# Scores taken from one pair transpose of q and k, the first units' low parts moved to ScalarE, and the last decisions moved by one slot

## Chip, core and metric

One core of a Trainium2 chip runs the whole program. The metric is device time in microseconds: the median of the runs of the kernel before is 1012.94 (1012.55 to 1014.28, three runs).

## The reference

Three layers, one after the other, all in float32 (the dense weights arrive as float64):

```
scores = q @ k.T / sqrt(64);  keep = (key < 4) | (0 <= query - key < 128)     # 4 sinks, window 128
x = softmax(where(keep, scores, -1e9)) @ v          # 4 batches, 8 heads, 768 positions, head size 64
x = (x @ w1) * (x @ w2) @ w3 @ w_out                # x: 3072 tokens x 512
logits = x @ w_gate + modality_bias[modality_id]; e = argmax(logits); gate = softmax(logits)[e]
out = gate * (relu(x @ w1[e]) @ w2[e])              # 8 experts, 512 -> 1024 -> 512, one per token
```

## The kernel before

Nearly every product is done in three passes of float32r: a high part (rounded by ScalarE as it copies) and a low part (the rest, by VectorE) of each operand, high x high, high x low and low x high.

**Start.** `startup_stream` loads the float64 weights with SP's DMA queue, builds float32 of them with three VectorE operations each (L182, L185, L188), transposes w3 on TensorE (L280) and multiplies w3 by w_out (L289). Attention of the first units runs between these.

**Attention.** The 3072 queries are 12 units of 256 (three to a batch), each with 4 pairs of heads: 48 steps n. For one n, `att_stream` yields five times: scores of the unit's first 128 queries, `a_scores(n, 0)`; sink weights and transposed P of n-1, `a_sk` and `a_pt`; q of n+1, `a_tq` and `a_swap`; scores of the second 128 queries; P times V of n-1, `a_pv`, and k of n+1, `a_tk`. Before a transpose, `a_split` lays the high and low part of a head side by side, so that one 128x128 transpose gives 64 rows of high part over 64 of low part; `a_swap` makes a copy with these halves exchanged. A score is then two products over 128 rows: (high, low) with (high, low), and the swapped pair with the same (L441). q takes four transposes and k four (L396, L415). What is kept of the previous unit's k lies in `carry`, and the sinks' k in `ksk`. P is divided by its sum on VectorE (L468). P times V (L531) is in full float32 and writes 64 output rows for one head and the other 64 for its partner. `defer` puts a VectorE step one yield later (`tick`).

**Dense layer.** `moe1_stream` takes two units at a time, six groups: L703 for x @ w1 and x @ w2, L691 for the product with w3 x w_out. During group g, attention of group g+1 and routing of group g-1's units run between: `route` is a generator of sixteen dot products on VectorE (L764) and the bookkeeping after them, among which five small matmuls (L786 to L790) wait for the one-hot rows of L775. How fast it is stepped is the `due` line of `front`.

**Experts.** `back` works through slots of 512 tokens. `decide` finds on VectorE, in some 16 tiny operations, which expert has most tokens left; SP reads the answer into registers and then issues the loads of token numbers (L846) and of the expert's weights (L868, L870), all on one queue. Four slots are decided early, in the last dense group; two more and one of 128 tokens are decided when all tokens are routed, at slot 2 (`pos == N_EARLY - 2`). A slot is `stage1` (L912), then four `stage2` (L949); within the latter stand the next slot's `w1_piece` splits and its transposes (L899).

A scheduler sets the order of each engine's instructions from the program's order, its own costs and the waits; engines then run their lists strictly in order.

Of the kernel before, what the change touches and what calls it, by code (L numbers as in the profile page):

```python
# [26 lines left out]
def attention_moe_moe_kernel(ctx, tc, q, k, v, w1, w2, w3, w_out, mod_id, w_gate, mod_bias, e_w1, e_w2, out,  # L27
                             n_sink, window, dbg=None):
    nc = tc.nc
# [16 lines left out]
    banded = n_sink == NS and window == 128  # L46

# [46 lines left out]
    neg_r = const.tile([128, 128], F32R, name="neg_r")  # L94
    cur_i = const.tile([128, 128], I32, name="cur_i")
# [12 lines left out]
    ksk = const.tile([128, H, NS], F32R, name="ksk")  # L108
# [3 lines left out]
    def consts_early():  # L112
# [5 lines left out]
        nc.vector.tensor_scalar(out=neg_r, in0=idf, scalar1=-1.0, scalar2=None, op0=ALU.mult)  # L118
        nc.gpsimd.memset(tmp, 1.0)
# [217 lines left out]
    carry = {}  # L337
    xb = mm.tile([128, NP, 2, 3, UNIT], F32R, tag="xb", bufs=1, name="xb")

    def a_load(n):  # L340
        u, p = divmod(n, NP)
        b, c = divmod(u, NC)
        hs = slice(2 * p, 2 * p + 2)
        qn = att.tile([128, 2, 2, D], F32, tag="qn", bufs=2, name="qn")
        kn = att.tile([128, 2, 2, D], F32, tag="kn", bufs=2, name="kn")
        for src, dst in ((q, qn), (k, kn)):
            for j in range(2):
                s0 = c * UNIT + j * 128
                nc.sync.dma_start(out=dst[:, :, j], in_=src[b, hs, s0:s0 + 128, :].rearrange("h s d -> s h d"))
        nat[n] = (qn, kn)  # L350

    def a_load_v(n):
# [3 lines left out]
        vn = att.tile([128, 3, 2, D], F32, tag="vn", bufs=2, name="vn")  # L356
# [4 lines left out]
        if c == 0 and p == 0:  # L361
            for kind in range(3):
                for h in range(2):
                    r = kind * 32 + h * NS
                    nc.sync.dma_start(out=vst[r:r + NS, :, h * D:(h + 1) * D],
                                      in_=v[b].rearrange("(p h) s d -> h s p d", h=2)[h, 0:NS])
# [7 lines left out]
    def a_split(n):  # L374
        qn, kn = nat.pop(n)
        qs = att.tile([128, 4, 2, D], F32R, tag="qs", bufs=1, name="qs")
        ks = att.tile([128, 4, 2, D], F32R, tag="ks", bufs=1, name="ks")
        qf = qn.rearrange("p h j d -> p (h j) d")
        kf = kn.rearrange("p h j d -> p (h j) d")
        nc.scalar.activation(out=qs[:, :, 0, :], in_=qf, func=ACTF.Copy, scale=1.0 / float(D) ** 0.5)  # L380
        nc.scalar.activation(out=ks[:, :, 0, :], in_=kf, func=ACTF.Copy)

        def low_parts():
            nc.vector.scalar_tensor_tensor(out=qs[:, :, 1, :], in0=qf, scalar=1.0 / float(D) ** 0.5,
                                           in1=f32(qs[:, :, 0, :]), op0=ALU.mult, op1=ALU.subtract)
            nc.vector.tensor_tensor(out=ks[:, :, 1, :], in0=kf, in1=f32(ks[:, :, 0, :]), op=ALU.subtract)

        stt["low", n] = defer(low_parts)
        stt["s", n] = (qs, ks)

    def a_tq(n):
        qs, ks = stt["s", n]
        stt.pop(("low", n))()
        tp = ps_t.tile([128, 4, 128], F32R, tag="t", name="tq")
        for i in range(4):
            nc.tensor.transpose(out=tp[:, i, :], in_=qs[:, i].rearrange("p a d -> p (a d)"), identity=idr)  # L396
        qT = att.tile([128, 4, 128], F32R, tag="qT0", bufs=2, name="qT")
        nc.scalar.activation(out=qT, in_=f32(tp), func=ACTF.Copy)
        stt["q", n, 0] = qT
        stt["tq", n] = tp  # L400

    def a_swap(n):
        qW = att.tile([128, 4, 128], F32R, tag="qT1", bufs=2, name="qW")
        tp = stt.pop(("tq", n))
        for x in range(2):
            nc.scalar.activation(out=qW[x * D:(x + 1) * D], in_=f32(tp[(1 - x) * D:(2 - x) * D]), func=ACTF.Copy)
        stt["q", n, 1] = qW

    def a_tk(n):
        u, p = divmod(n, NP)  # L410
        b, c = divmod(u, NC)
        qs, ks = stt.pop(("s", n))
        tp = ps_t.tile([128, 4, 128], F32R, tag="t", name="tk")
        for i in range(4):
            nc.tensor.transpose(out=tp[:, i, :], in_=ks[:, i].rearrange("p a d -> p (a d)"), identity=idr)  # L415
        kT = att.tile([128, 2, 3, KW], F32R, tag="kT", bufs=1, name="kT")
        for h in range(2):
            nc.scalar.activation(out=kT[:, h, 1:3, NS:KW], in_=f32(tp[:, 2 * h:2 * h + 2, :]), func=ACTF.Copy)
        if c == 0:
            nc.gpsimd.tensor_copy(out=ksk[:, 2 * p:2 * p + 2, :], in_=f32(kT[:, :, 1, NS:2 * NS]))  # L420
        s0 = 0 if c else 1
        nc.gpsimd.tensor_copy(out=kT[:, :, s0:3, 0:NS],
                              in_=f32(ksk[:, 2 * p:2 * p + 2, :]).unsqueeze(2).to_broadcast([128, 2, 3 - s0, NS]))
        if c:
            nc.vector.tensor_copy(out=kT[:, :, 0, NS:KW], in_=f32(carry[p]))
        if c < NC - 1:
            cr = att.tile([128, 2, 128], F32R, tag=f"carry{p}", bufs=1, name="carry")
            nc.vector.tensor_copy(out=cr, in_=f32(kT[:, :, 2, NS:KW]))
            carry[p] = cr
        stt["k", n] = kT  # L430

    def a_scores(n, j):
        u, p = divmod(n, NP)
        b, c = divmod(u, NC)
        kT = stt["k", n]
        sp = ps_s.tile([128, 2, 512], F32, tag="s", name="sp")
        blk0 = c == 0 and j == 0
        s0 = 1 if blk0 else j
        for h in range(2):
            for part in range(2):  # L440
                nc.tensor.matmul(out=sp[:, h, 0:2 * KW], lhsT=stt["q", n, part][:, 2 * h + j, :],  # L441
                                 rhs=kT[:, h, s0:s0 + 2, :].rearrange("p a b -> p (a b)"),
                                 start=(part == 0), stop=(part == 1))
# [8 lines left out]
        else:  # L452
            nc.vector.copy_predicated(out=sp[:, :, NS:KW], mask=cur_i.unsqueeze(1).to_broadcast([128, 2, 128]),
# [10 lines left out]
        def norm():  # L464
            r = st[:, 2]
            nc.vector.tensor_scalar(out=st[:, 1], in0=st[:, 1], scalar1=1.0e-9, scalar2=None, op0=ALU.add)
            nc.vector.reciprocal(out=r, in_=st[:, 1])
            nc.vector.tensor_tensor(out=P[:, j, :, lo:KW], in0=P[:, j, :, lo:KW],  # L468
# [4 lines left out]
    def a_sk(n):  # L473
# [6 lines left out]
        xp = ps_x.tile([128, 2, 256], F32, tag="x", name="xp")  # L480
        stt["x", n] = xp
# [5 lines left out]
        for j in range(j0, 2):  # L487
# [3 lines left out]
                                    op=ALU.subtract)  # L491
            nc.tensor.transpose(out=xp[0:96, 1, j * 128:(j + 1) * 128].bitcast(F32R), in_=psk[:, j, :], identity=idr)
# [25 lines left out]
    def a_pv(n):  # L518
# [10 lines left out]
        for x, (vj, cols, pm) in enumerate(spans):  # L529
            for h in range(2):  # L530
# [4 lines left out]
                         start=False, stop=True, skip_group_check=True)  # L535
        xh, xl = xb[:, p, 0, u % 3], xb[:, p, 1, u % 3]
        nc.scalar.activation(out=xh, in_=xp[:, 0], func=ACTF.Copy)  # L537
        defer(lambda: nc.vector.tensor_tensor(out=xl, in0=xp[:, 0], in1=f32(xh), op=ALU.subtract))
        stt.pop(("k", n)); stt.pop(("q", n, 0)); stt.pop(("q", n, 1))

    NN = NU * NP

    att_done = [0]
    ATT_STEPS = 5

    def att_stream():
        a_load(0)
        a_load_v(0)
        a_load(1)
        a_vsink(0)  # L550
        a_split(0)
        a_tq(0)
        a_swap(0); yield
        a_tk(0); yield
# [660 lines left out]
```

## Time and profile before

| | us |
|---|---|
| median of the runs shown | 1012.94 |
| profiled execution, its own time | 1017.59 |
| span of its profile | 1015.9 |
| dense groups 0 to 5 begin at | 129.3, 227.6, 332.3, 432.8, 531.5, 632.5 |
| slots 0 to 5 begin at | 708.7, 754.6, 800.7, 855.3, 901.2, 947.0 |
| last matmul begins | 1003.4 |

The page gives busy time and idle time; a timeline gives the start and length of runs of like instructions. The length of a TensorE row has a modelled end, so that rows overlap: what a piece of TensorE work costs is read from one start to the next start. In L531's rows a float32 matmul stands as two instructions, one for each pass over its columns.

### The profile page before, as it was taken

The numbers are of one execution on the slowest core, as the hardware profiler recorded it, in microseconds if no ns is written. First come the engines' busy times: TensorE is split into PE (matmuls) and PEld (weight loads), VectorE is DVE, ScalarE is ACT, GpSimd is POOL, SyncE is SP. The second block draws the span as 40 slices with busy tenths as digits, with TensorE's granted clock in tenths as the row PEclk, the third lists the DMA queues.
The fourth block names the chain that finished last, engine by engine and source line by source line (L and its number), as shares of the span: only waits on it lengthen the run. The fifth ranks groups of instructions, "written<-read, shape, count | busy, mean of one in ns | idle before, by whom it ended". The sixth has DMA issues, their size and how long they took to land. (4 is left out here: it accounts for less than half of the span.)

```text
span 1015.9 us, 16038 instructions
## 1 busy us (share of the span) xinstructions
PE 956.0 (94%) x4976; PEld 752.5 (74%) x4976; DVE 644.0 (63%) x1968; ACT 515.8 (51%) x1354; POOL 218.0 (21%) x460
## 2 busy tenths in 40 slices
PE   4899799999999999999999999999999997999995
PEld 2667578867786778678867886778888886888884
DVE  7788796489638963895489639847934354343432
ACT  3689665576447644774576445314433414343433
POOL 1232312113223221222122222222031222021010
PEclk9899999999999999999999999999999998999998
DMA  8665624112202220222022200452445306343331
GB/s 262 188 171 167 188 69 131 23 45 63 58 19 49 58 55 19 56 61 52 16 50 59 58 9 16 129 80 63 145 166 117 133 13 236 125 146 117 122 116 52
DMA packets 125417, 94.05 MB, mean 93 GB/s; under 512 B 96712, under 2 KB 105160, under 8 KB 125201
## 3 DMA queue, kind: packets, MB, share of 16 engines
q1 hardware_dynamic: 120560, 80.12, 28.3%
q0 software_dynamic: 4768, 12.88, 4.2%
q8 instruction: 40, 0.66, 0.3%
q14 instruction: 49, 0.39, 0.2%
HBM read 80.14 MB, written 13.09 MB: 92 GB/s over the span
## 5 line engine op out<-in xcount | busy, mean ns | idle before, releaser
L703 PE MATMUL ab<-xb,wab 128*128 128x512 f32 x1152 | 291.0, 397 | 0.4 <-DVE g L713 0.3
L703 PEld LDWEIGHTS ab<-xb,wab 128*128 128x128 f32 x1152 | 210.6, 189 | 41.9 <-ACT xb L537 1.2
L949 PE MATMUL x<-w 128*128 128x512 f32 x600 | 143.1, 396 | 0.0
L764 DVE CUSTOM_DVE_ANT_0 junk<-rows,wgb 128x512 bf16<-128x512 f32 x192 | 134.8, 702 | 1.5 <-ACT rows L751 0.6
L949 PEld LDWEIGHTS x<-w 128*128 128x128 f32 x600 | 113.1, 190 | 23.7 <-DVE w L196 0.3
L691 PE MATMUL x2p<-w3o,gh 128*128 128x512 f32 x384 | 128.2, 407 | 0.0
L461 ACT ACTIVATE P<-sp,st 128x132 f32<-128x132 f32 (+1 forms) x192 | 69.2, 368 | 40.4 <-DVE st L459 26.4
L196 DVE TENSOR_TENSOR w<-wst,w 128x512 fp32r<-128x512 f32 x112 | 71.5, 683 | 25.1 <-ACT w L195 25.1
L513 POOL TENSOR_SCALAR_AFFINE_SELECT ptp<-ptf 128x512 f32<-128x512 f32 (+1 forms) x96 | 63.7, 688 | 107.8 <-ACT ptf L508 107.8
L691 PE MATMUL x2p<-w3o,gl 128*128 128x512 f32 x192 | 76.4, 400 | 0.0
L691 PEld LDWEIGHTS x2p<-w3o,gh 128*128 128x128 f32 x384 | 66.9, 188 | 11.8 <-ACT gh L680 1.9
L912 PE MATMUL ab<-w,w 128*128 128x512 f32 x288 | 75.1, 396 | 0.0
L916 DVE SCALAR_TENSOR_TENSOR w<-ab,w 128x512 fp32r<-128x512 f32 x48 | 33.1, 690 | 65.6 <-ACT w L915 65.4
L195 ACT ACTIVATE w<-wst 128x512 fp32r<-128x512 f32 x112 | 63.5, 628 | 20.9 <-DMA wst<-in_moe_w_dram 20.9
L912 PE MATMUL ab<-w 128*128 128x512 f32 x288 | 74.0, 392 | 0.0
L953 POOL DMA_INDIRECT out_dram<-late,ti x25 | 25.6, 1026 | 217.1 <-ACT late L952 193.0
L680 ACT ACTIVATE gh<-g 128x256 fp32r<-128x256 f32 x96 | 39.9, 415 | 63.0 <-DVE g L710 48.1
L710 DVE TENSOR_TENSOR g<-ab,bs 128x256 f32<-128x256 f32 x48 | 20.2, 421 | 76.6 <-PE ab L703 76.5
L485 POOL CAST psk<-P 128x16 fp32r<-128x16 f32 (+1 forms) x96 | 23.7, 276 | 202.1 <-DVE P L468 149.6
L915 ACT ACTIVATE w<-ab 128x512 fp32r<-128x512 f32 x48 | 28.8, 599 | 74.5 <-PE ab L912 74.1
L912 PEld LDWEIGHTS ab<-w,w 128*128 128x128 f32 x288 | 54.0, 188 | 13.0
L912 PEld LDWEIGHTS ab<-w 128*128 128x128 f32 x288 | 54.0, 188 | 12.1
(195 smaller groups left out, 1685.7 us busy)
## 6 DMA issues: line engine op xcount, KB each, us to landing
wst<-in_moe_w_dram SPq DMA_DIRECT2D x56, 512.0 KB
f64st<-in_moe_w_dram SPq DMA_DIRECT2D x32, 512.0 KB
vn<-in_v_dram SPq DMA_DIRECT2D x128, 64.0 KB
xs<-rows SPq DMA_DIRECT2D x12, 513.0 KB
qn<-in_q_dram SPq DMA_DIRECT2D x96, 64.0 KB
kn<-in_k_dram SPq DMA_DIRECT2D x96, 64.0 KB
f64st<-in_moe_w_out_dram SPq DMA_DIRECT2D x8, 512.0 KB
wgb<-wgt SPq DMA_DIRECT2D x1, 2048.0 KB
```

The lines of the kernel that those rows point to most:

```text
L195: nc.scalar.activation(out=hi, in_=src, func=ACTF.Copy)
L196: lo_eng.tensor_tensor(out=lo, in0=src, in1=f32(hi), op=ALU.subtract)
L461: nc.scalar.activation(out=P[:, j, h, lo:KW], in_=sp[:, h, lo:KW], func=ACTF.Exp, bias=st[:, 0, h:h + 1], accum_out=st[:, 1, h:h + 1])
L513: nc.gpsimd.affine_select(out=parts[:, a, i0:2].rearrange("p j h q -> p (j h) q"), in_=full[:, 2 * i0:4], pattern=[[0, 4 - 2 * i0], [sign, ...
L680: nc.scalar.activation(out=gh, in_=g, func=ACTF.Copy)
L691: nc.tensor.matmul(out=x2p[t], lhsT=a[:, sl], rhs=b_, start=(f == 0 and i == 0), stop=(f == KF - 1 and i == 2))
L703: nc.tensor.matmul(out=bank[nm].rearrange("p (u t) -> p u t", u=2), lhsT=a, rhs=b_, start=(kk == 0 and i == 0), stop=(kk == KD - 1 and i = ...
L764: nc.vector.tensor_tensor_reduce(out=junk, in0=rows[:, t, 0:DM], in1=wgb[0][:, e, :], scale=1.0, scalar=0.0, op0=ALU.mult, op1=ALU.add, ac ...
L912: nc.tensor.matmul(out=hp, lhsT=a[:, fs], rhs=b_, start=(kk == 0 and i == 0), stop=(kk == KD - 1 and i == 2))
L915: nc.scalar.activation(out=h[:, 0], in_=hp, func=ACTF.Relu)
L916: nc.vector.scalar_tensor_tensor(out=h[:, 1], in0=hp, scalar=0.0, in1=f32(h[:, 0]), op0=ALU.max, op1=ALU.subtract)
L949: nc.tensor.matmul(out=op, lhsT=a[:, ts], rhs=b_, start=(f == 0 and i == 0), stop=(f == KF - 1 and i == 2))
```

## The change

- q and k of a pair of heads are loaded side by side and transposed as they are, in float32: four transposes for one n in place of eight. Row 0 to 63 of the result is one head, 64 to 127 the other. ScalarE copies the high parts, VectorE takes the low parts from PSUM, one yield later; `carry`, `ksk` and the swapped copy go, and k stays in a ring of three blocks of 128 keys (`ring`).
- A score is three products over 64 rows for each head; the heads' products stand in turn, on rows 0 to 63 and 64 to 127. In a batch's first block they are 132 columns wide and not 264.
- For the first eight n (`FEW`) the low parts come from TensorE: minus the high part is added to the bank and ScalarE copies the rest. ScalarE also divides these P.
- `a_skT` takes the sink weights' transpose out of `a_sk` and puts it one yield later. V has three buffers and not two.
- The first q, k and v loads stand behind two float64 loads and not ten; the sinks' v loads come later.
- In the last dense group routing is stepped as in the others; the decisions of slots 1 to 3 start at 47000 and not 20000 (in the units of `front`'s plan).
- The last slots are decided inside slot 3's stage 1.

```diff
-        for i in range(4):
-            nc.tensor.transpose(out=tp[:, i, :], in_=qs[:, i]..., identity=idr)
+        for x, src in enumerate((qn, kn)):
+            for j in range(2):
+                nc.tensor.matmul(out=tp[:, 2 * x + i], lhsT=src[:, j], rhs=idf, is_transpose=True, ...)
+        nc.scalar.activation(out=qh, in_=tp[:, 0:2], func=ACTF.Copy, scale=scale)
+        nc.scalar.activation(out=kr[:, 0, blocks, NS:KW], in_=tp[:, 2:4], func=ACTF.Copy)
+        def low_parts():
+            if n < FEW:
+                nc.tensor.matmul(out=tp[:, 0:2], lhsT=negq_r, rhs=qh, start=False, stop=True, ...)
+                nc.tensor.matmul(out=tp[:, 2:4], lhsT=neg_r, rhs=kr[:, 0, blocks, NS:KW], start=False, stop=True, ...)
...
-        for h in range(2):
-            for part in range(2):
-                nc.tensor.matmul(out=sp[:, h, 0:2 * KW], lhsT=stt["q", n, part][:, 2 * h + j, :],
-                                 rhs=kT[:, h, s0:s0 + 2, :].rearrange("p a b -> p (a b)"),
+        for i, (a, b_) in enumerate(((qh, 0), (ql, 0), (qh, 1))):
+            for h in range(2):
+                hp = slice(h * D, (h + 1) * D)
+                nc.tensor.matmul(out=sp[:, h, 0:nk].rearrange("p (a b) -> p a b", b=KW), lhsT=a[hp, j, :],
+                                 rhs=kr[hp, b_, blocks, :], start=(i == 0), stop=(i == 2))
...
-                    due = min(t, 18000) / 420
+                    due = min(t, 46000) / 1100
...
-            if pos == N_EARLY - 2:
+                    if pos == N_EARLY - 1 and f == 2:
```

In a dense group, TensorE's list had the following (pt: transposes of P; tq: transposes of q; the two sp rows at the end stand there once more, for the second head):

```order
L492 MATMUL xp_3681<-idr_92,psk_107 96x128 x2
L504 MATMUL pt_3690<-idf_91,P_3423 128x128 x4
L703 MATMUL ab_3700<-xb_109,wab_1894 128x512 x12
L396 MATMUL tq_3720<-idr_92,qs_3635 128x128 x4
L691 MATMUL x2p_3089<-w3o_1412,gh_3605 128x512 x2
L691 MATMUL x2p_3089<-w3o_1412,gl_3606 128x512
L691 MATMUL x2p_3090<-w3o_1412,gh_3605 128x512 x2
L691 MATMUL x2p_3090<-w3o_1412,gl_3606 128x512
L441 MATMUL sp_3737<-kT_3585,qT_3516 128x264
L441 MATMUL sp_3737<-kT_3585,qW_3518 128x264
```

At the like place it now has these (each sp row is one product of both heads; a third such row, with qh and the low part of k, follows):

```order
L515 MATMUL pt_3059<-idf_91,P_2806 128x128 x4
L714 MATMUL ab_3069<-xb_109,wab_1509 128x512 x9
L395 MATMUL tqk_3100<-idf_91,qn_2793 128x128 x2
L395 MATMUL tqk_3100<-idf_91,kn_2794 128x128 x2
L503 MATMUL xp_3109<-idr_92,psk_107 96x128 x2
L702 MATMUL x2p_2894<-w3o_743,gh_2963 128x512 x2
L702 MATMUL x2p_2894<-w3o_743,gl_2964 128x512
L702 MATMUL x2p_2895<-w3o_743,gh_2963 128x512 x2
L702 MATMUL x2p_2895<-w3o_743,gl_2964 128x512
L442 MATMUL sp_3125<-ring_584,qh_2884 128x264 x2
L442 MATMUL sp_3125<-ring_584,ql_2885 128x264 x2
```

The sinks' transpose stood ahead of P's and now stands behind the next q and k, twelve dense matmuls later. In the whole list a score group stands next to a P times V group, with nothing between, at 22 places before and at 16 now, and the score groups lie in 98 pieces before and in 101 now.

SP's list at the last decisions had the token numbers of the last slot (tk), the loop count (tri), and then the first w1 load of slot 3:

```order
L846 DMA tk_9877<-tab0_70 128x1
L846 REGISTER_ALU
L846 DMA tk_9877<-tab1_71 128x1
L1168 TENSOR_LOAD tri_9881
L1168 ISA x2
L868 ISA
L868 DMA wst_9923<-in_moe2_w1_dram 128x1024
```

Now slot 3's last w1 load and its first w2 load stand ahead of the first register read of the decisions (dri):

```order
L879 DMA wst_9293<-in_moe2_w1_dram 128x1024
L881 ISA
L881 DMA wst_9346<-in_moe2_w2_dram 128x2x512
L850 TENSOR_LOAD dri_9496
L850 ISA x2
L851 TENSOR_LOAD dri_9496
L851 ISA x2
```

The four w1 loads of slot 3 moved ahead of the decisions; its w2 loads 2 to 4 follow the register reads, then the token numbers, then slot 4's w1. VectorE's list keeps the decisions' own operations where they were, behind slot 2's stage 1.

At the program's start SP's queue had ten weight loads ahead of the first q, of which these are the last four, and two more ahead of k:

```order
L172 DMA f64st_227<-in_moe_w_out_dram 128x1024
L172 DMA f64st_229<-in_moe_w_out_dram 128x1024
L172 DMA f64st_293<-in_moe_w_out_dram 128x1024
L172 DMA f64st_295<-in_moe_w_out_dram 128x1024
L349 DMA qn_167<-in_q_dram 128x2x64 x2
L172 DMA f64st_349<-in_moe_w_out_dram 128x1024
L172 DMA f64st_351<-in_moe_w_out_dram 128x1024
L349 DMA kn_168<-in_k_dram 128x2x64 x2
L359 DMA vn_173<-in_v_dram 128x2x64 x2
```

Now two stand there:

```order
L176 DMA f64st_128<-in_moe_w3_dram 128x1024
L176 DMA f64st_130<-in_moe_w3_dram 128x1024
L353 DMA qn_132<-in_q_dram 128x2x64 x2
L353 DMA kn_133<-in_k_dram 128x2x64 x2
L364 DMA vn_138<-in_v_dram 128x2x64 x2
L176 DMA f64st_141<-in_moe_w_out_dram 128x1024
L176 DMA f64st_143<-in_moe_w_out_dram 128x1024
```

The first unit's q, k and v moved ahead of eight to ten weight loads.

## Rows read from the trace of the kernel before

**Rows 1.** The page: busy time, share of the span, instructions.

```profile
PE 956.0 (94%) x4976; PEld 752.5 (74%) x4976; DVE 644.0 (63%) x1968; ACT 515.8 (51%) x1354; POOL 218.0 (21%) x460
```

**Rows 2.** Windows: length, busy PE, PEld, DVE, ACT, POOL; then clock, DMA.

```profile
0.00:70.00 70.00, 50.11 (x242) 36.01 (x243) 55.46 (x130) 41.16 (x105) 14.14 (x40) 0.95 0.71 215
227.50:332.00 104.50, 101.34 (x587) 78.12 (x585) 72.88 (x259) 60.80 (x181) 27.62 (x66) 1.00 0.20 48
708.60:1003.80 295.20, 289.56 (x1304) 236.64 (x1302) 135.85 (x310) 113.16 (x208) 48.70 (x57) 0.99 0.41 128
```

**Rows 3.** Who waited for whom, TensorE: total, times, longest.

```profile
PE xp L492 <- POOL psk L488: 14.5, 23, 4.9
PE w3tp L280 <- DVE w L188: 10.7, 4, 7.4
PE x L899 <- DVE w L196: 5.6, 1, 5.6
PE sp L441 <- POOL kT L422: 3.6, 5, 1.1
PE rk L786 <- DVE oh L775: 2.6, 1, 2.6
```

**Rows 4.** Timeline of TensorE, q transposes and a score group: start, length.

```profile
302.14 0.45 PE L396 MATMUL tq<-idr,qs 128*128 128x128 f32 x4
302.43 0.70 PE L691 MATMUL x2p<-w3o,gh 128*128 128x512 f32 x2
302.96 0.40 PE L691 MATMUL x2p<-w3o,gl 128*128 128x512 f32 x1
...
303.89 0.29 PE L441 MATMUL sp<-kT,qT 128*128 128x264 f32 x1
...
304.38 0.63 PE L691 MATMUL x2p<-w3o,gh 128*128 128x512 f32 x2
304.85 0.39 PE L691 MATMUL x2p<-w3o,gl 128*128 128x512 f32 x1
```

**Rows 5.** The same timeline, transposes of P in float32.

```profile
311.39 0.61 PE L504 MATMUL pt<-idf,P 128*128 128x128 f32 x4
311.76 0.71 PE L691 MATMUL x2p<-w3o,gh 128*128 128x512 f32 x2
312.31 0.40 PE L691 MATMUL x2p<-w3o,gl 128*128 128x512 f32 x1
```

**Rows 6.** The same timeline, a P times V group between dense matmuls.

```profile
305.54 0.40 PE L691 MATMUL x2p<-w3o,gl 128*128 128x512 f32 x1
305.87 0.65 PE L531 MATMUL xp<-ptp,vn 128*64 128x256 f32 x2
306.44 0.74 PE L691 MATMUL x2p<-w3o,gh 128*128 128x512 f32 x2
307.02 0.40 PE L691 MATMUL x2p<-w3o,gl 128*128 128x512 f32 x1
```

**Rows 7.** Groups of instructions, VectorE in attention: busy, mean ns.

```profile
L468 DVE TENSOR_TENSOR P<-P,st 128x264 f32<-128x264 f32 (+1 forms) x96 | 42.5, 443 | 2.0
L384 DVE SCALAR_TENSOR_TENSOR qs<-qn,qs 128x256 fp32r<-128x256 f32 x48 | 21.1, 439 | 8.2 <-ACT qs L380 8.1
L538 DVE TENSOR_TENSOR xb<-xp,xb 128x256 fp32r<-128x256 f32 x48 | 20.1, 420 | 22.7 <-ACT xb L537 21.9
```

**Rows 8.** Windows, as rows 2: two stretches behind TensorE stalls.

```profile
121.50:125.00 3.50, 3.50 (x12) 2.68 (x12) 0.00 (x0) 0.86 (x2) 1.22 (x2) 0.51 0.87 296
660.90:664.30 3.40, 3.16 (x12) 2.58 (x12) 3.05 (x23) 0.60 (x1) 2.79 (x3) 0.50 0.40 30
```

**Rows 9.** Windows, as rows 2: stage 2 of slots 1 and 2.

```profile
777.00:800.60 23.60, 23.60 (x114) 19.65 (x113) 8.09 (x14) 8.77 (x16) 6.11 (x6) 1.00 0.51 175
823.10:855.20 32.10, 26.46 (x114) 21.77 (x113) 16.14 (x59) 10.03 (x18) 9.20 (x18) 0.89 0.49 164
```

**Rows 10.** Timeline of SP's queue, slot 3's w1 loads.

```profile
836.94 7.36 SPq L868 DMA_DIRECT2D wst<-in_moe_w_dram  x4
```

More of the change, by code (lines that the diff above doesn't have):

```diff
@@ L1 @@
+import math
 from contextlib import ExitStack
@@ L94, in attention_moe_moe_kernel @@
     neg_r = const.tile([128, 128], F32R, name="neg_r")
+    negq_r = const.tile([128, 128], F32R, name="negq_r")
     cur_i = const.tile([128, 128], I32, name="cur_i")
@@ L336, in attention_moe_moe_kernel @@
     stt = {}
-    carry = {}
+    ring = []
     xb = mm.tile([128, NP, 2, 3, UNIT], F32R, tag="xb", bufs=1, name="xb")
@@ L360, in a_load_v, with a_load_sinks @@
         stt["v", n] = vn
-        if c == 0 and p == 0:
-            for kind in range(3):
-                for h in range(2):
-                    r = kind * 32 + h * NS
-                    nc.sync.dma_start(out=vst[r:r + NS, :, h * D:(h + 1) * D],
-                                      in_=v[b].rearrange("(p h) s d -> h s p d", h=2)[h, 0:NS])
+        if n and c == 0 and p == 0:
+            a_load_sinks(b)
+    def a_load_sinks(b):
+        for kind in range(3):
+            for h in range(2):
+                r = kind * 32 + h * NS
+                nc.sync.dma_start(out=vst[r:r + NS, :, h * D:(h + 1) * D],
+                                  in_=v[b].rearrange("(p h) s d -> h s p d", h=2)[h, 0:NS])
     def a_vsink(b):
@@ L372, in a_vsink @@
         stt["vsk", b] = vsk
[L374 to L394, printed above, removed]
-        for i in range(4):
[L396 to L407, printed above, removed]
@@ L434, in a_scores @@
         b, c = divmod(u, NC)
-        kT = stt["k", n]
+        if j == 0:
+            stt.pop(("low", n))()
+        kr = ring[p]
+        qh, ql = stt["q", n]
         sp = ps_s.tile([128, 2, 512], F32, tag="s", name="sp")
+        cur = (2 * c + j) % 3
         blk0 = c == 0 and j == 0
-        s0 = 1 if blk0 else j
-        for h in range(2):
-            for part in range(2):
-                nc.tensor.matmul(out=sp[:, h, 0:2 * KW], lhsT=stt["q", n, part][:, 2 * h + j, :],
-                                 rhs=kT[:, h, s0:s0 + 2, :].rearrange("p a b -> p (a b)"),
-                                 start=(part == 0), stop=(part == 1))
+        wrapped = cur == 0 and not blk0
+        blocks = slice(0, 1) if blk0 else slice(0, 3, 2) if wrapped else slice(cur - 1, cur + 1)
+        nk = KW if blk0 else 2 * KW
+        for i, (a, b_) in enumerate(((qh, 0), (ql, 0), (qh, 1))):
+            for h in range(2):
+                hp = slice(h * D, (h + 1) * D)
+                nc.tensor.matmul(out=sp[:, h, 0:nk].rearrange("p (a b) -> p a b", b=KW), lhsT=a[hp, j, :],
+                                 rhs=kr[hp, b_, blocks, :], start=(i == 0), stop=(i == 2))
         if j == 0:
@@ L467, in norm @@
             nc.vector.reciprocal(out=r, in_=st[:, 1])
+            if n < FEW:
+                for h in range(2):
+                    nc.scalar.activation(out=P[:, j, h, lo:KW], in_=P[:, j, h, lo:KW], func=ACTF.Copy,
+                                         scale=r[:, h:h + 1])
+                return
             nc.vector.tensor_tensor(out=P[:, j, :, lo:KW], in0=P[:, j, :, lo:KW],
@@ L491, in a_sk, with a_skT @@
                                     op=ALU.subtract)
+    def a_skT(n):
+        c = n // NP % NC
+        j0 = 0 if c else 1
+        xp = ps_x.tile([128, 2, 256], F32, tag="x", name="xp")
+        stt["x", n] = xp
+        for j in range(j0, 2):
             nc.tensor.transpose(out=xp[0:96, 1, j * 128:(j + 1) * 128].bitcast(F32R), in_=psk[:, j, :], identity=idr)
@@ L1128, in back @@
                     route_step()
[L1129 to L1137 removed]
+                    if pos == N_EARLY - 1 and f == 2:
+                        while route_step():
+                            pass
+                        for x in range(N_LATE + 1):
+                            slots.append(Slot(SLOT if x < N_LATE else 128, NT, mem))
+                            slots[-1].decide()
+                        cnt = trips(p2a_pool[0])
+                        order += list(range(N_EARLY, len(slots)))
             nx = slots[order[pos + 1]] if pos + 1 < len(order) else None
```

114 lines of the change are left out of this document (62 added, 52 removed).

## Prediction

> **What bounds the kernel now.** I read the page's busy times first, then TensorE's waits, then windows by stage, and last the timeline of TensorE around attention. The page shows TensorE busy for 956.0 us of a span of 1015.9, far ahead of VectorE with 644.0 and ScalarE with 515.8 [rows 1]. The reader is to see in the windows where this differs by stage: in a dense group TensorE is busy for 101.34 of 104.5 us, behind the routing 289.56 of 295.2, and in the first 70 us only 50.11 while VectorE has 55.46 [rows 2]. So from 70 us on an edit counts by what TensorE itself does with it, or by the stall it makes or ends; ScalarE and VectorE work saved there is worth nothing of its own. In the waits the reader sees that few stalls carry a name: 14.5 us for the sinks' transpose L492, 10.7 for the first converted weights, 5.6 at the expert transposes L899, 3.6 for GpSimd's copies of the sinks' k, 2.6 for a routing matmul [rows 3].
>
> **Transposes.** In the timeline four transposes of q and the two L691 behind them go from 302.14 to 302.96, 0.82 us; two L691 behind a score group go from 304.38 to 304.85, 0.47 [rows 4]. So four float32r transposes cost 0.35, and the two groups of a step n cost 0.70. The float32 kind that takes their place is there in L504: from 311.39 to 312.31 are 0.92, less 0.47 is 0.45 for four [rows 5]. One such group replaces two of the others: 0.25 less for each of 48 n, **-12 us**. Each sits between dense matmuls, so it counts in full.
>
> **Scores.** Here the sign of the dense groups is decided. A group of four products over 128 rows goes from 303.89 to 304.38, 0.49, or 0.12 for each, and the two matmuls after it are at their usual 0.47: it has no tail [rows 4]. Now there are six products over 64 rows. Two things are not in this trace: whether the heads' products run at the same time, and what a change between 128 and 64 rows costs. The nearest rows are P times V, which splits the array by output columns. Going in, the L691 at 305.54 lasts 0.33 to the next start, not 0.23: +0.10. Inside, 305.87 to 306.44 are 0.57, where two float32 passes of 256 columns should take 0.44 by L504's 0.11 for 128: +0.13. Coming out, two L691 go from 306.44 to 307.02, 0.58: +0.11 [rows 5, 6]. A round trip costs 0.34. The score weights are 128 columns wide where these are 64, and the way out, with 128 columns to load, shows 0.11 for them; I add 0.05 and take 0.39. If the pairs overlap, three products of 0.12 follow: 0.36 + 0.39 = 0.75 in place of 0.49, +0.26 for 80 groups, 21 us. The 16 groups of a batch's first block stream half the columns, but their weights must still come in; by the 0.09 of one float32r transpose that is 0.27 + 0.39 = 0.66, +0.17, 3 us. By the order, 16 groups share a change with a P times V group beside them, at some 0.2 less each, and five more pieces cost 0.39 each: -1. Sum **+22 us**. From both sides: if the change of rows costs nothing, the group is 0.36, and the sum is 80 x -0.13 + 16 x -0.22 = -14. If the pairs do not overlap and the change costs as above, it is 6 x 0.12 + 0.39 = 1.11, +0.62 for 80 groups and some +0.44 for 16: +56, less 1. I take the middle value because the rows of L531 are the only ones in which the array is split.
>
> The Trainium skill, TensorEngine Tiling (Array Packing), section Tiling Modes, says under its key properties that a change of tiling mode drains the engine while tiles of one mode work side by side. L531's rows agree for columns, by their 0.10 and 0.11 [rows 6]; no row here shows it for rows of the array, and by this rule the sum is the +22 above.
>
> **First units and the start.** For eight n TensorE gets two correction matmuls for q and k and one for the output, 256 columns each: 24 x 0.12 by L441's rate, **+3**. VectorE loses, for each of these n, the two divisions of P (0.443 each), the low parts of q and k (0.439 and about as much), and the output's (0.420) [rows 7]: 2.2 us x 8 = 17 us, in a stretch in which it is busy for 55 of 70 us. TensorE stands idle for 20 of the first 70 us [rows 2], but 7.4 of this ends only when the first weights are converted [rows 3], and most of the rest is the chain load, convert, transpose, which stays. q, k and v now come behind two weight loads, so attention fills some of the gaps. I take **-4**; bounds 0 and -12, since the idle time less the 7.4 is some 12.
>
> **Waits of the attention.** L492's 14.5 us end when GpSimd has copied the sinks' weights. The transpose now stands one yield and some twelve dense matmuls later (2.8 us at 0.23), and 22 of its 23 waits are 0.4 on average; the longest, 4.9, also had TensorE at half its clock (0.51, the 1.2 GHz level) from 121.5 to 125, worth half of 3.4 [rows 3, 8]. I take 13 and 1.7: **-14.7**. The wait for GpSimd's sinks of k, 3.6, goes for two units in three, since the ring keeps them, and is a yield earlier in the others: **-3**. What is late next is the one PSUM bank that holds the transposes, which VectorE now frees by its low parts where ScalarE did: the transposes of P and the routing matmuls queue behind that. The nearest rows are the waits of L441 and L786, 3.6 and 2.6 in all [rows 3]. I put **+3** for it, bounds 0 and +17 (all of what the two terms above give). What goes of `carry` copies, splits and swaps on VectorE, ScalarE and GpSimd lay beside TensorE's dense matmuls and counts nothing.
>
> **Last dense group.** L786 waited 2.6 us for VectorE, which had the routing's dot products and the w1 splits in one heap, and the clock then stood at 0.50 from 660.9 to 664.3 [rows 3, 8], 1.7 more. At the pace of the other groups, where no such wait is listed, both should go: 4.3, of which I take **-3**. The later decisions of slots 1 to 3 block SP's queue until VectorE has decided; slot 0's second weights queue behind, and have all of its stage 1, some 22 us, to land.
>
> **Last slots.** Stage 2 of slot 2 lasts 32.1 us, that of slot 1 23.6 [rows 9]. In it TensorE waits 5.6 us for VectorE's splits, which wait for slot 3's w1; SP issues that only at 836.94, behind the decisions' register reads and token loads [rows 3, 10]. The rest is the clock, 0.89 in this window. The order now has these loads ahead, so all of it goes: **-8.5**. The decisions' reads now stand ahead of slot 3's w2 loads, which have its stage 1 as cover, and ahead of slot 4's w1, needed a slot later.
>
> **Sum.** -12 + 22 + 3 - 4 - 14.7 - 3 + 3 - 3 - 8.5 = -17. The profiled execution took 1017.6 us by its own time, 4.7 above the median of the runs shown; 1017.6 - 17.2 - 4.7 = 995.7, and I say **996**.
>
> **Rivals.** *The change of rows is free* (chance 0.22). The scores then give -14 in place of +22: 960. For it speaks that the two heads use different banks and rows, and that nothing about columns has to hold for rows; against it, that every group of L531 pays. The Trainium skill, TensorE: Matmul & The Clock Gate, part 3 on packing small matmuls, gives a pack the time of one matmul and some 4 ns for each further tile and names no cost of entering; by that rule the time would be this rival's. L531 pays on entering [rows 6], and no run here shows a pack by rows.
>
> *The heads' products run one after the other* (0.09). The scores cost +55: 996 + 33 = 1029, **slower**. For it speaks only that no row shows an overlap by rows; against it, that the heads' products stand alternately. It decides from the point where a group costs more than the other terms give back: these are -39, over 96 groups 0.41, so from 0.90 us a group on, against 0.75 in my forecast.
>
> *The waits come back under other names* (0.09). The bank of the transposes, freed by VectorE, stalls TensorE for what the POOL waits cost before: +17 in place of +3 gives 1010, about no change. For it speaks that VectorE is 70% busy in a dense group [rows 2]; against it, that the low parts have two yields.
>
> The forecast keeps 0.60; its own range, from the bounds of the start's term and the bank's, is 986 to 1007. **Range: 956 to 1010.** This leaves out most of the slow rival and the lower half of the free one. A difference below 0.2%, some 2 us, is about what a measurement of this kernel can't tell from none. Faster by more, below 1010.9: the forecast nearly whole, the free rival and a part of the third, 0.85; within, 0.06; slower, 0.09.
>
> **What would show it.** A score group of about 0.75 us from its first start to the next dense one, with the L702 or L714 before and behind it stretched by 0.10 and 0.11, is the forecast; 0.36 without a stretch is the free rival; six starts 0.12 apart the slow one. The two heads' starts should lie some ns apart. L503 should be gone from the waits, the windows of stage 2 should all be 23.6 us, the clock should drop at neither the last group's routing nor slot 2. The first dense group should begin by 122, not 129.3. I am wrong if the dense groups take less than 97 or more than 104 us (100.5 now, the third), or if a wait for the bank of the transposes, over 5 us in all, stands in the list.

## The result and the profile after

The changed kernel takes 997.07 us (median, 996.09 to 998.05) against 1013.24 for the kernel before in the same measurement: a ratio of 0.984, 95% interval 0.9822 to 0.9857. 996 had been forecast. Its profiled execution took 997.91 us, 19.7 less than that of before.

The page's row of busy times (as [rows 1]), of the changed kernel:

```profile
PE 955.2 (96%) x5000; PEld 729.6 (73%) x5000; DVE 623.8 (63%) x1865; ACT 419.9 (42%) x1170; POOL 204.5 (21%) x412
```

TensorE is busy for as long as before (956.0); of the 19.7 us, 18.9 are its idle time (59.9 to 41.0 of the span). ScalarE has 96 us less work, beside a TensorE that is busy for 96% of the span; no gain below is put down to that.

Windows by stage, with the columns of [rows 2]: the stretch up to 70 us, one dense group, all that lies behind the routing.

```profile
0.00:70.00 70.00, 53.01 (x258) 36.25 (x259) 49.82 (x115) 40.62 (x121) 10.74 (x39) 0.95 0.69 213
223.90:328.30 104.40, 101.03 (x582) 74.30 (x581) 69.85 (x234) 40.70 (x135) 24.50 (x54) 1.00 0.22 46
698.60:984.10 285.50, 285.50 (x1303) 234.34 (x1301) 136.15 (x310) 112.71 (x207) 53.82 (x65) 1.00 0.47 134
```

The dense group is as long as before (104.4 against 104.5). Behind the routing TensorE now has no idle time at all, and this stretch alone is 9.2 us shorter: 285.9 from its first matmul to the end of the last one against 295.1. The other stages, by the first dense matmul of each group: the start 129.3 to 124.1 (-5.2), groups 0 to 4 together 503.2 to 504.2 (+1.0), the last group 76.2 to 70.3 (-5.9). The four give -19.3: groups 0 to 4, where most of the new scores and transposes lie, gained nothing, and the whole gain lies ahead of them and behind them.

TensorE's waits, as [rows 3]:

```profile
PE xp L503 <- POOL psk L492: 8.2, 16, 0.8
PE w3tp L284 <- DVE w L192: 8.2, 2, 7.6
PE pt L515 <- DVE P L474: 2.4, 4, 0.7
PE w3o_acc L293 <- DVE wo L200: 2.2, 1, 2.2
PE sp L442 <- ACT P L462: 1.5, 4, 0.6
...
PE x2p L702 <- ACT gh L691: 0.5, 1, 0.5
```

L503 is the L492 of before, which waits for psk, the sinks' weights that GpSimd copies: 14.5 has become 8.2 and has not gone. The waits of L899, L786 and for kT are gone. No wait at a transpose into the transposes' bank is over 2.4 in all, and those 2.4 end when VectorE has divided P.

The timeline of TensorE around a score group, and at the transposes of q and k (L395); [rows 4 to 6] are the places before.

```profile
296.71 0.40 PE L702 MATMUL x2p<-w3o,gl 128*128 128x512 f32 x1
297.03 0.39 PE L442 MATMUL sp<-ring,qh 64*128 64x264 f32 x2
297.26 0.29 PE L442 MATMUL sp<-ring,ql 64*128 64x264 f32 x2
297.38 0.29 PE L442 MATMUL sp<-ring,qh 64*128 64x264 f32 x2
297.60 0.73 PE L702 MATMUL x2p<-w3o,gh 128*128 128x512 f32 x2
298.16 0.40 PE L702 MATMUL x2p<-w3o,gl 128*128 128x512 f32 x1
...
314.29 0.38 PE L395 MATMUL tqk<-idf,qn 128*128 128x128 f32 x2
314.50 0.38 PE L395 MATMUL tqk<-idf,kn 128*128 128x128 f32 x2
314.64 0.70 PE L702 MATMUL x2p<-w3o,gh 128*128 128x512 f32 x2
```

The L702 ahead of the scores lasts 0.32 to the next start, some 0.10 over its usual 0.23; the group lasts 0.57, where three pairs of 0.12 would be 0.36; the two L702 behind it last 0.56, 0.11 over their usual 0.46. The trace has the two matmuls of a pair start 3 to 4 ns apart (median). Over all groups between dense matmuls, with the two stretches counted in, the median is 0.77 us for 264 columns (0.75 forecast) and 0.685 for 132 (0.66 forecast).

Windows of the stretch that held the cold clock of [rows 8], and of stage 2 of slots 1 and 2 ([rows 9]):

```profile
116.00:124.10 8.10, 8.10 (x52) 5.91 (x51) 8.03 (x18) 4.70 (x13) 1.98 (x3) 1.00 0.64 182
...
766.60:790.20 23.60, 23.60 (x113) 19.68 (x112) 8.08 (x13) 8.77 (x16) 6.08 (x6) 1.00 0.53 176
812.60:836.10 23.50, 23.50 (x113) 19.65 (x112) 15.78 (x63) 7.79 (x15) 3.55 (x4) 1.00 0.75 100
```

TensorE does not stand at 116 any more and stays at 2.4 GHz (granted clock 1.00). Both stages 2 are equal, as forecast, and the clock is 1.00 behind the routing too.

### The profile page after: what moved, and what is told of

Same layout as the page of the kernel before. It is cut to its first block, busy times and chain, and to the rows that moved or that the text cites. A ratio compares the mean times of both kernels' runs of the same rounds, so it can differ in the third digit from the quotient of the medians.

```text
span 996.2 us, 15561 instructions
## 1 busy us (share of the span) xinstructions
PE 955.2 (96%) x5000; PEld 729.6 (73%) x5000; DVE 623.8 (63%) x1865; ACT 419.9 (42%) x1170; POOL 204.5 (21%) x412
## 5 line engine op out<-in xcount | busy, mean ns | idle before, releaser
L775 DVE CUSTOM_DVE_ANT_0 junk<-rows,wgb 128x512 bf16<-128x512 f32 x192 | 138.8, 723 | 3.5 <-ACT rows L762 2.3
L702 PE MATMUL x2p<-w3o,gh 128*128 128x512 f32 x384 | 129.2, 412 | 0.5 <-ACT gh L691 0.5
L524 POOL TENSOR_SCALAR_AFFINE_SELECT ptp<-ptf 128x512 f32<-128x512 f32 (+1 forms) x96 | 66.4, 715 | 101.6 <-ACT ptf L519 101.3
L200 DVE TENSOR_TENSOR w<-wst,w 128x512 fp32r<-128x512 f32 x112 | 71.3, 685 | 11.4 <-ACT w L199 11.2
L702 PE MATMUL x2p<-w3o,gl 128*128 128x512 f32 x192 | 77.4, 403 | 0.0
L702 PEld LDWEIGHTS x2p<-w3o,gh 128*128 128x128 f32 x384 | 66.0, 188 | 15.6 <-issue 2.3
L442 PE MATMUL sp<-ring,qh 64*128 64x264 f32 (+1 forms) x384 | 60.8, 329 | 2.5 <-ACT P L462 1.5
```

Source lines behind the costliest of these rows:

```text
L200: lo_eng.tensor_tensor(out=lo, in0=src, in1=f32(hi), op=ALU.subtract)
L442: nc.tensor.matmul(out=sp[:, h, 0:nk].rearrange("p (a b) -> p a b", b=KW), lhsT=a[hp, j, :], rhs=kr[hp, b_, blocks, :], start=(i == 0), st ...
L524: nc.gpsimd.affine_select(out=parts[:, a, i0:2].rearrange("p j h q -> p (j h) q"), in_=full[:, 2 * i0:4], pattern=[[0, 4 - 2 * i0], [sign, ...
L702: nc.tensor.matmul(out=x2p[t], lhsT=a[:, sl], rhs=b_, start=(f == 0 and i == 0), stop=(f == KF - 1 and i == 2))
L775: nc.vector.tensor_tensor_reduce(out=junk, in0=rows[:, t, 0:DM], in1=wgb[0][:, e, :], scale=1.0, scalar=0.0, op0=ALU.mult, op1=ALU.add, ac ...
```

## The experiments

Each is set against the kernel before, run in the same measurement, by its ratio; the changed kernel's is 0.984.

**Do the heads' products overlap, and by what.** First the order:

```
-        for i, (a, b_) in enumerate(((qh, 0), (ql, 0), (qh, 1))):
-            for h in range(2):
+        for h in range(2):
+            for i, (a, b_) in enumerate(((qh, 0), (ql, 0), (qh, 1))):
```

> The changed kernel with the six score products in another order: all three of head 0, then all three of head 1, on the same rows, banks and weights. The theory (the two heads' products of a pair run side by side, and a round trip to 64 rows and back costs some 0.40 on top): a group of 264 columns goes from 0.77 to 1.0 or 1.1 us, since only the third product of head 0 can still lie beside one of head 1 (5 or 6 times 0.12 in place of 3, and the 0.40), some +0.24 to +0.36 for 80 groups and half of that for 16: +21 to +32, 1018 to 1029 us. The rival (the pair gives nothing, the group is as long as its six weight loads and the two changes): the time stays within 2 us of 997.

Measured: 999.48 us, ratio 0.9858 (0.9841 to 0.9874), not to be told from the changed kernel. The timeline of a score group in it:

```profile
299.08 0.40 PE L702 MATMUL x2p<-w3o,gl 128*128 128x512 f32 x1
299.41 0.40 PE L442 MATMUL sp<-ring,qh 64*128 64x264 f32 x2
299.63 0.30 PE L442 MATMUL sp<-ring,ql 64*128 64x264 f32 x2
299.75 0.29 PE L442 MATMUL sp<-ring,qh 64*128 64x264 f32 x2
299.98 0.73 PE L702 MATMUL x2p<-w3o,gh 128*128 128x512 f32 x2
```

The theory's number fell: the group is 0.77 as before. But the starts still come in pairs, now 10 ns apart in place of 3 to 4, though three products of one head stand in the queue ahead of the other's. The rival would give the same time, so the next kernel takes the overlap away:

```
-                ... lhsT=a[hp, j, :], rhs=kr[hp, b_, blocks, :], ...
+                ... lhsT=a[0:D, j, :], rhs=kr[0:D, b_, blocks, :], ...
```

> The changed kernel, in which the products of both heads read rows 0 to 63 (left out: the scores of each pair's second head, which become a copy of the first's). Number, size and order of the products, banks and everything else are kept; only the two products of a pair can't lie side by side. Theory (the pairs do overlap, whatever the order in the queue, and starts 3 to 10 ns apart mean this): six products of 0.12 in place of three, the group of 264 columns at about 1.1 us in place of 0.77, some 0.34 x 80 + 0.17 x 16 = +30, 1027 us. Rival (the starts are an artefact of the records, the six run one after the other in any case): 997, with a group of 0.77.

Measured: 1022.53 us, ratio 1.0102 (1.0083 to 1.012). The timeline of a group in it:

```profile
306.75 0.40 PE L702 MATMUL x2p<-w3o,gl 128*128 128x512 f32 x1
307.08 0.50 PE L442 MATMUL sp<-ring,qh 64*128 64x264 f32 x2
307.43 0.40 PE L442 MATMUL sp<-ring,ql 64*128 64x264 f32 x2
307.67 0.40 PE L442 MATMUL sp<-ring,qh 64*128 64x264 f32 x2
307.99 0.73 PE L702 MATMUL x2p<-w3o,gh 128*128 128x512 f32 x2
```

Now the six start one after the other, the middle ones 0.12 apart, and the group is 1.125 us (median), 25 us in all (the theory's sum was 30). So the pairs do run side by side, in either order of the queue. Both kernels also give the price of the change of rows: 0.767 less three times 0.12, and 1.125 less six times 0.12, is 0.40 each time. It lies on both sides: some 0.10 in the dense matmul ahead and 0.10 more than usual behind the first product or pair, then 0.09 more behind the last one and 0.11 in the dense matmuls after it.

**Taking the change of rows away.** `qh` now holds high over low part for one head and low over high for the other, `ql` the reverse, `ring` as `qh`:

```
+        if n >= NP * NC:
+            at = [slice(h * D, (h + 1) * D) for h in range(2)]
+            for h in range(2):
+                nc.scalar.activation(out=qh[at[h], h], in_=tp[at[h], 0:2], func=ACTF.Copy, scale=scale)
...
+        for h in range(2 if n >= NP * NC else 0):
+            for i, a in enumerate((qh, ql)):
+                nc.tensor.matmul(..., lhsT=a[:, h, j, :], rhs=kr[:, h, blocks, :], ...)
```

> The changed kernel, but from the second batch on (36 of 48 n) the scores are four products over 128 rows as in the kernel before, with the high and low parts of each head stacked; the pair transposes stay. ScalarE and VectorE fill the stacks, eight and four instructions on half of the partitions in place of two and two; q, k have one buffer each and v two, for room, and q, k are loaded some 3 us later. The theory (what the scores cost more than before is the change of rows, 0.77 against 0.49 for 264 columns, 0.68 against some 0.45 for 132): 60 x 0.28 + 12 x 0.2 = 19 us less, 978 us, and the L702 before and behind a group no longer stretched. Rival one (the weights' loads and not the change of rows make the group long): 997. Rival two (ScalarE and VectorE are now late with the stacks, and score groups wait in the list): 997 or more.

Measured: 991.15 us, ratio 0.9781 (0.9764 to 0.9797): 6 us less than the changed kernel, between theory and rivals. The timeline of a group in it:

```profile
294.53 0.40 PE L733 MATMUL x2p<-w3o,gl 128*128 128x512 f32 x1
294.76 0.28 PE L468 MATMUL sp<-ring,qh 128*128 128x264 f32 x1
...
295.13 0.29 PE L468 MATMUL sp<-ring,ql 128*128 128x264 f32 x1
295.26 0.63 PE L733 MATMUL x2p<-w3o,gh 128*128 128x512 f32 x2
```

The L733 ahead lasts 0.23, the group 0.50: the stretches are gone and the group has its 0.49, which was the theory's mechanism. What became of the 19 us shows when TensorE's time in groups 1 to 4 is split up (from each matmul's start to the next one's; what a dense matmul beside attention lasts over 0.2285 is put to the attention):

| us in groups 1 to 4 | before, 227.6 to 632.5 | changed, 223.9 to 628.3 | stacked_rows, 221.0 to 620.6 |
|---|---|---|---|
| scores (groups) | 36.3 (63) | 45.1 (62) | 36.8 (63) |
| transposes of q, k | 24.7 | 11.4 | 13.8 |
| transposes of P | 23.4 | 25.6 | 24.2 |
| transposes of the sinks | 7.8 | 9.5 | 10.8 |
| P times V, and the sinks' V | 46.4 | 46.7 | 46.2 |
| dense and the rest | 266.3 | 266.0 | 267.7 |
| sum | 404.9 | 404.2 | 399.6 |

A score group costs 0.576, 0.727 and 0.584 on average, a difference of 0.14 to 0.15 and not of 0.28: a group over 128 rows that has P times V right behind it (8 of the 63 before) lasts mostly 0.68 inside and not 0.49, in both kernels, where one over 64 rows keeps its 0.56, and some had a wait in them. Of the 8.3 us that the scores gave back, 4.6 arrive in the sum: 5.4 went to the transposes of q, k and of the sinks and to dense matmuls that waited, and 1.9 came back at the transposes of P and at P times V. How much of this the single buffers made was not tried apart.

**The wait for the sinks' weights.** Three kernels turn on it.

```
-                a_sk(n - 1); a_pt(n - 1); yield
+                a_sk(n - 1); a_skT(n - 1); a_pt(n - 1); yield
...
-            if n:
-                a_skT(n - 1)
```

> The changed kernel with the sinks' transposes back right behind GpSimd's copies, ahead of the transposes of P. The theory (this distance took away most of the 14.5 us that TensorE waited for GpSimd at this line, and 8.2 are left in the changed kernel): 5 to 8 us more, 1002 to 1005, with 13 to 16 us of waits for psk in the list. The rival (the waits became shorter because the units of batch 0 no longer divide P on VectorE, or because of chance in the order): within 2 us of 997, psk's waits at 8 to 9.

Measured: 1004.4 us, ratio 0.9902 (0.9885 to 0.9918), and in its waits:

```profile
PE xp L503 <- POOL psk L492: 15.6, 21, 1.7
```

As the theory said. But none of these is over 1.7, where the kernel before had one of 4.9 ahead of its first dense group: that one does not come back with the distance. Moving the transposes further away, on top of stacked_rows, gave nothing more:

```
-            if n:
-                a_skT(n - 1)
             yield
             a_scores(n, 1)
+            if n:
+                a_skT(n - 1)
```

> The kernel stacked_rows, with the sinks' transposes one yield later still, behind the second score group. The wait for GpSimd's copies of the sinks' weights is 8.3 us there (17 times, the longest 0.9). Theory (a wait ends by distance, and nothing but P times V stands behind it): 5 to 8 us less, 983 to 986, psk under 2 us in the list. Rival (the transposes' copy on ScalarE is now late for P times V's last matmul, or the order puts the transposes at the same place as before): 989 to 992, with a wait for pskT, or psk still at 8.

Measured: 989.71 us, ratio 0.9771 (0.9756 to 0.9786), which does not differ from stacked_rows; 7.7 us of psk are left. The rival held. Its median is the lowest of the study. What these waits end on is one step further back. GpSimd's waits in the changed kernel:

```profile
POOL psk L489 <- DVE P L474: 145.0, 28, 11.4
```

GpSimd copies only when VectorE has divided P, and the routing's products stand ahead of that. So:

```
-            if n < FEW:
+            if FEW:
                 for h in range(2):
                     nc.scalar.activation(out=P[:, j, h, lo:KW], ...
```

> The changed kernel with P divided on ScalarE for all 48 n and not for the first eight alone; nothing else differs. GpSimd's copies of the sinks' weights wait for VectorE's division of P for 145 us there, 28 times, the longest 11.4, behind the routing's products. Theory (the 8.2 us that TensorE waits for psk and the 2.4 for P at its transposes are VectorE's lateness): both fall below 3 in all, 5 to 9 us less, 988 to 992. Rival (ScalarE, with some 12 us more in each dense group, is now the one that is late: waits for gh, bs, P's exponentials): 996 or more.

Measured: 992.41 us, ratio 0.9801 (0.977 to 0.9831), 4.7 us under the changed kernel by the medians, at the theory's edge; the two intervals still overlap by a little, so the waits say more than the time. TensorE's waits in it:

```profile
PE pt L515 <- ACT P L471: 2.5, 6, 0.8
PE xp L503 <- POOL psk L492: 2.3, 6, 0.7
```

psk fell from 8.2 to 2.3, and the wait for VectorE's P is gone; ScalarE's P has 2.5 in its place. Together with the stacks it does not pay:

> The kernel stacked_rows_sinks_later with P divided on ScalarE for all n. Theory (as for divide_on_scalar): psk's 7.7 us of waits fall below 3, 4 to 8 us less than its 990, 982 to 986. Rival (ScalarE, 58 of 100 us busy in a dense group of that kernel, has no room for 12 more at the moments that count): 989 to 994, with waits for ScalarE's copies in the list.

Measured (the two edits above in one kernel): 996.64 us, ratio 0.9845 (0.9817 to 0.9873), 7 us more than without the division on ScalarE, and more than the rival said. The window of one dense group in it, and one of its waits ahead of P times V (L573):

```profile
421.00:521.60 100.60, 97.77 (x532) 74.62 (x531) 73.59 (x246) 69.01 (x221) 23.28 (x53) 1.00 0.21 46
...
412.44 0.37 ACT L536 ACTIVATE pskT<-xp 96x256 fp32r<-96x256 f32 x1
412.91 0.65 PE L573 MATMUL xp<-ptp,vn 128*64 128x256 f32 x4 [1.02 <-issue]
```

ScalarE is busy for 69 of 100.6 us; psk is at 4.1 in place of 7.7, but P times V and the scores, counted as in the table between 125 and 700 us (without the sinks' V), take 104.7 us in place of 97.1. The waits ahead of P times V alone went from 2.2 us to 6.9. Five of them, 3.6 us, end some 0.1 us behind ScalarE's copy of the transposed sinks' weights (pskT), as the one shown, though only one of them (0.3) stands under its name in the waits; the others end behind GpSimd's ptp. So ScalarE is late for half of this, as the rival had it; the other half was not followed further.

**The first units and the loads.**

```
-    FEW = 2 * NP if math.frexp(QDIV)[0] == 0.5 else 0
+    FEW = 0
```

> The changed kernel with the eight first n treated as all others: VectorE makes their low parts and divides P, TensorE is rid of 24 matmuls of 256 columns. Theory (VectorE, 55 of the first 70 us busy, holds the start back): the first dense group begins at 126 to 129 in place of 124.1, in all 2 to 5 us more, 999 to 1002. Rival (the start goes by the chain load, convert, transpose, and by it alone; the 24 matmuls are then 3 us for nothing): 994 to 997.

Measured: 1001.97 us, ratio 0.989 (0.9871 to 0.9909). The time is the theory's, the place is not: the first dense group begins at 124.0, but it takes 104.8 us in place of 99.8. TensorE's waits between 100 and 230 us in this kernel:

```profile
PE xp L503 <- POOL psk L492: 4.7, 4, 3.4
```

The changed kernel has 1.4 there, the longest 0.5. It is a wait of the kind of the long one before, in a later place, and the clock behind it is low again (0.55 from 134.2 to 138.0 us). The next kernel goes further than the kernel before did: it takes out `f64_ahead(2)`, and SP's queue then has q, k and v of the first n ahead of all weight loads, where the changed kernel has two weight loads ahead of q and the kernel before had ten:

> The changed kernel with q, k, v of the first n loaded ahead of the first two weight loads again. Theory (the first converted weights are waited for, 7.6 us at the first transpose of weights, and six loads ahead of theirs make them later): that wait grows by 1 to 2 us and the first dense group begins at 125 to 126 in place of 124.1, 998 to 999 us. Rival (the loads use different queues and do not delay one another, attention's head start pays for the rest): that wait stays at 7.6 and the time within 1 us of 997.

Measured: 999.85 us, ratio 0.9873 (0.9843 to 0.9904), not to be told from the changed kernel; in its profile the first dense group begins 1.2 us later. The wait at the first weights got shorter (8.2 to 6.8 in all), so the theory's path is wrong; q's own loads were waited for 3.4. It is not the order of the kernel before, so what the step from ten loads to two is worth was not tried apart.

**The routing's pace.** Undone in the changed kernel (the edit below), and made alone in the kernel before (the same edit the other way round):

```
-                early += [(47000 + 1500 * i, next_early) for i in range(N_EARLY - 1)]
+                early += [(20000 + 3000 * i, next_early) for i in range(N_EARLY - 1)]
...
-                    due = min(t, 46000) / 1100
+                    due = min(t, 18000) / 420
```

> The changed kernel with the routing's products of the last group in a heap again and the decisions of slots 1 to 3 early, as before. Theory (the last group gained 5.9 us, 76.2 to 70.3, by it: VectorE's heap made a routing matmul wait and the clock fell): 4 to 6 us more, 1001 to 1003, the last group at 74 to 76 us, a wait for L775 at the routing matmul and a stretch at half the clock behind it. Rival (the last group gained by its attention or by what the heap no longer delays in the group before): within 2 us of 997.

> The kernel before with this one edit: the routing's products of the last group at the pace of the others, the decisions of slots 1 to 3 late. Theory one (the heap makes the wait of 2.6 us at the routing matmul L786 and the 1.7 of half a clock behind it; that undoing the edit in the changed kernel did not bring them back is chance, its VectorE being less loaded): the wait goes, the last group falls from 76.2 to about 72, 1009 us. Theory two (the place of that wait is set by the attention's tail and the other work around it, the pace matters little in either kernel): 1012 to 1014, the last group at 75 or more, with a wait at L786 of its own or another.

Measured: 998.88 us, ratio 0.9864 (0.9844 to 0.9884), and 1011.44 us, ratio 0.9995 (0.9975 to 1.0015); neither differs from its base. In the profiles the first has its last group at 69.9 us (70.3 in the changed kernel), and its routing matmul waits 0.3 us. The second has it at 73.3 in place of 76.2, with L786's wait gone and these left in that group:

```profile
PE xp L492 <- POOL psk L488: 1.1, 1, 1.1
PE xp L531 <- POOL ptp L513: 0.8, 1, 0.8
```

So the wait of 2.6 and the cold clock end with the pace alone, and also without it, by the rest of the change; that VectorE's lighter load is what does it in the rest is argued, not shown. Of the other 3 us of the last group, 1.9 are these two waits of the attention's tail, which the changed kernel no longer has. That the pace alone is worth its 2.9 us stands in one profile only.

**The last slots.** The decisions back behind stage 1 of the third slot:

```
-                    if pos == N_EARLY - 1 and f == 2:
+            if pos == N_EARLY - 2:
```

> The changed kernel with the decisions of the last slots behind stage 1 of the third slot, as before. The theory (the third slot's stage 2 waited for the next slot's w1, which stood behind the decisions in SP's queue): 8 to 9 us more, 1005 to 1006, with stage 2 of the third slot at 31 to 32 us in place of 23.6 and a drop of the clock in it. The rival (the gain behind the routing came from the routing's pace, which leaves fewer steps for this place): 997 to 1000.

Measured: 1007.11 us, ratio 0.9944 (0.9927 to 0.996), some 10 us more, 1 over the theory. Stage 2 of the third slot as a window, and its wait:

```profile
812.70:843.60 30.90, 25.61 (x113) 21.14 (x113) 16.15 (x59) 10.02 (x18) 8.74 (x18) 0.89 0.49 168
```

```profile
PE x L910 <- DVE w L200: 5.3, 1, 5.3
```

## Why the prediction came out right

Sum against sum, the forecast was -17.2 from profile to profile and -19.7 came. That it came so near is in part luck: two of its largest terms were wrong in size and the errors cancelled. Groups 1 to 4 show it; they hold two thirds of the steps n. The forecast's terms for transposes, scores and kT make some +5 there, its waits for psk some -5 (6.1 of the 14.5 us lie there), the bank +2. The table has -4.5 for transposes of q and k and scores together, +1.7 for the sinks' transposes with their waits, and +2.2 for the transposes of P. Both sums are near zero. The third dense group took 101.5 us, inside the 97 to 104 named as a sign; the gain came in the start, the last group and the last slots.

*Transposes, -12, and scores, +22.* The mechanism and the single groups are as forecast: 0.45 for four transposes, 0.77 and 0.685 for the scores, stretches of 0.10 and 0.11. But I took the price of before from groups between dense matmuls alone. By the table a score group cost 0.576 on average, 0.15 less than now: 96 times that is +14.5. The transposes of one n fell from 0.80 to 0.38 on average, -20 for 48. Their sum is -5.5 where I had +10; kT's -3 is contained in the -5.5, so that +7 is what it stands against.

*Waits of the attention, -14.7.* This step failed: "L503 should be gone", but 8.2 us are left, and with the 1.7 of cold clock the gain is 8. Of these, 6.6 are the long wait at 116 us (4.9) and its clock, which went because the first units no longer load VectorE (first_units_on_vector), and not by the distance. In groups 1 to 4 the wait did not fall; before and now:

```profile
PE xp L492 <- POOL psk L488: 6.1, 15, 0.8
PE xp L503 <- POOL psk L492: 6.9, 13, 0.8
```

Without the distance it is 9.8 there (sinks_transpose_back), and 7 us more are spent in the whole kernel. So the rest of the change had made this wait longer, which was not tried apart, and the distance took about that much back. What is left hangs on VectorE's division of P (divide_on_scalar). I had named GpSimd as what ends the wait and had not asked what GpSimd waits for.

*Bank of the transposes, +3.* No wait over 2.4 us stands there; the transposes of P cost 2.2 more in four groups, of which 1.9 are waits for P's division and not for the bank.

*Start, +3 and -4.* The first dense group came at 124.1, not by 122. The -5.2 are no more than the stall at 116 and its cold clock (6.6), which I had among the waits. The first units are worth 4.9, and by first_units_on_vector it shows in the first dense group. What the earlier loads gave, no run shows.

*Last group, -3, and last slots, -8.5.* -5.9 and -9.2. The slots' mechanism is shown; the pace is worth some 3 in one profile of the kernel before and nothing that could be measured in the changed one; the tail of the attention has 1.9 of the other 3.

*The rivals.* The change of rows is not free: 0.40 a group, by two kernels. The Trainium skill, TensorE: Matmul & The Clock Gate, part 3, lets further tiles of a pack start some 4 ns apart, and the pairs' 3 to 4 ns agree; it has no such price, and the measurement decides. The rule of the drain on a change of mode, weighed in the forecast (TensorEngine Tiling (Array Packing), section Tiling Modes, of the Trainium skill), fits for rows too in that a change has a price, 0.40 us the round trip; that a drain is what costs it, no trace here shows. The heads' products don't run one after the other; where they are made to, the group is at 1.125 us, past the 0.90 from which I said it turns slower, and the kernel is slower than before. The waits did not come back under other names, except for 2.4 us for VectorE's P. The forecast's own range was added up wrongly: its bounds for the start and the bank give 985 to 1014, not 986 to 1007.

## What to carry to other kernels

Price a group of small matmuls over all its places, not where it stands cleanest: beside other small groups and with its waits it cost 0.08 us more than the clean 0.49, which, with the new group a little under its clean price, halved the price of the change. Follow a wait one step past the engine that releases it: here more distance gave nothing once VectorE, behind GpSimd, was late. By these figures, splitting the array by rows pays only where what the pairs save is large against 0.40 us for each round trip; with three pairs of 0.12 us, four products over all rows were cheaper by 0.28 us between dense matmuls, though in the whole kernel only a third of that arrived.

## What was not expected of the hardware

Products for two row halves run side by side even when three for one half stand in the queue ahead of the first for the other: pairs started 10 ns apart in place of 3 to 4, and the group kept its 0.77 us. In the queue the weights came as qh, ql, qh for one head and then the same for the other; by the rows of heads_in_turn they started as qh twice, ql twice, qh twice. So across the two halves TensorE did not start its products in the order of its list, which is more than "strictly in order" in the description of the kernel before allows. Each half seems to take up its own products as they are issued; that the 10 ns are the issue of three in place of one is argued, not shown.
